# Weight sums issued one step ahead of their casts on GpSimd, in a two-branch kernel on one Trainium2 core

## The chip, the cores and the metric

The kernel runs on one core of one Trainium2 chip. The metric is the device time of one execution in microseconds (us). Five engines matter here: TensorE (PE) does the matrix products, VectorE (DVE) and ScalarE (ACT) the elementwise work on PSUM and SBUF, GpSimd (POOL) elementwise work on SBUF, and SyncE (SP) issues nearly all transfers. In the profile PEld is TensorE's weight load.

## The reference

The output is a sum of three things of shape 2048 x 512: the input, a spectral filter of its layer norm, and a mixture of 8 experts in which every expert is used (K = 8), so the routing only sets a weight per token and expert.

```python
xn = _layernorm(x)
X  = rfft2(xn) * (w_r + 1j * w_i);  A = irfft2(X)          # spectral branch, 2048 x 512
gates = softmax(xt @ wg)                                   # 8 gates per token, all kept
h = gelu(einsum("nd,edf->nef", xt, w1))                    # 8 experts, 512 -> 1792
y = einsum("nef,efd->ned", h, w2)                          # 1792 -> 512
out = x + A + einsum("ne,ned->nd", gates, y)
```

## The kernel before, in words

Precision is kept by splitting every operand of a product into a rounded high part and the remainder (low part). A high part is made by ScalarE (a cast, written CAST in the profile), the low part by a subtraction on VectorE or GpSimd that reads the source and the high part just written. A product is then three passes: high x low, low x high, high x high.

The hidden width of all experts together is cut into 56 chunks of 256. The first 8 chunks are computed plainly (`mm1`, `mm2`, lines 571 and 596) while the spectral branch runs in the background. The other 48 chunks are computed in 24 **pairs** by a Winograd-Strassen scheme, and it is this stage, from about 509 us to the end, that the change is about.

A pair `c` takes two chunks at once. Its first-layer weight, transfer `raw<-in_wa`, is cut in four blocks a11, a12, a21, a22; from these GpSimd makes four sums s1 = a21 + a22, s2 = s1 - a11, s3 (from a11 and a21) and s4 = a12 - s2 (`sums1`, line 736, through `pooled`, line 733). s3 is written over a21 and s4 over a12. Seven blocks a11, a12, s1, s2, s3, s4, a22 are then split: a cast on ScalarE and a low part on GpSimd (`split`, line 548). The tiles are called `ua..` and `us..`. The second-layer weight of the pair (`raw<-in_wb`, `sums2`, line 753) goes the same way into tiles `va..` and `vs..`.

A pair has two **units** `u = 2c + i`, one per half of the tokens (`i` = 0 and 1). In a unit, `layer1` computes seven products of weights and prepared inputs (`xr`), all by `product` at line 785, and between them ScalarE takes the gelu (line 808), VectorE adds partial results (814, 817) and multiplies by the gates (837), and the results are split again into tiles `hs` (cast 821, low part 824). The results of a unit are called h11, h12, h22 and s; their combinations feed the seven products of `layer2`, which run one unit later, in turn with the next unit's first-layer products. So in the steady state TensorE does 14 products of 12 matmuls per unit and 28 per pair. The first product of `layer2` is b22 x s4: it needs the split of h22 (the last but one of the unit's results) and the tile vs4.

The weights for the next pair of units are prepared in small steps spread over the seven rounds of a unit: in even units (`i` = 0) the v weights that this pair's `layer2` needs, in odd units the u weights of the next pair. `prepare` (line 771) is a generator; `weights(n)` (line 1096) advances it by a number of steps that a small table gives for round `n`, and each step does the sums and then the splits that the generator hands out:

```python
for step in items:
    for n, src in step:
        to[n] = pool.tile([P, 2, 2, FC], F32R, name=f"{tag}{n}")
        split(to[n], src.rearrange(...), nc.gpsimd)
    yield
```

The sums of a step stand directly ahead of the cast that reads them. The order of the instructions on each engine is a scheduler's, except where `pin` (line 545) holds it to the order in which the program was written; `strict` turns this on for the whole Strassen stage. ScalarE, VectorE, GpSimd and SyncE each work off their instructions in the order shown, so an instruction that waits holds up all behind it on that engine.

Of the kernel before, what the change touches and what calls it, by code (L numbers as in the profile page):

```python
# [11 lines left out]
F32 = mybir.dt.float32  # L12
# [16 lines left out]
F2 = 2 * FC  # L29
N2 = (E * NC - N1) // 2  # L30
# [64 lines left out]
def body(ctx: ExitStack, tc: tile.TileContext, io):  # L95
    nc = tc.nc
# [4 lines left out]
    plain, early = ExitStack(), ExitStack()  # L101
# [78 lines left out]
    last_pe, last_dve, last_act, last_pool, main_act, last_cast, last_sp = ([None] for _ in range(7))  # L180
# [361 lines left out]

    strict = False

    def pin(ins):
        return tc.keep_in_program_order(ins) if strict else ins

    def split(dst, src, eng=None):
        main_act[0] = pin(nc.scalar.copy(dst[:, 0], src)).ins  # L549
        return pin((eng or nc.vector).tensor_tensor(dst[:, 1], src, r32(dst[:, 0]), op=ALU.subtract)).ins  # L550
# [147 lines left out]
    bg, step1 = background(), iter(())  # L698
# [34 lines left out]
    def pooled(dst, a, b, op):  # L733
        pin(nc.gpsimd.tensor_tensor(dst, a, b, op=op))  # L734

    def sums1(raw, tp, early):

        a11, a12, a21, a22 = (raw[:, i * F2 : (i + 1) * F2] for i in range(4))
        s1, s2 = (tp.tile([P, F2], F32, name=n) for n in ("s1", "s2"))
        yield [("a11", a11)]  # L740
        pooled(s1, a21, a22, ALU.add)
        yield [("a12", a12)]
        pooled(s2, s1, a11, ALU.subtract)
        yield [("s2", s2)]
        pooled(a21, a11, a21, ALU.subtract)
        if early:
            yield [("s3", a21)]
        yield [("s1", s1)]
        pooled(a12, a12, s2, ALU.subtract)
        yield [("s4", a12)]  # L750
        if not early:
            yield [("s3", a21)]
        yield [("a22", a22)]

    def sums2(raw, tp, c):

        a11, a12, a21, a22 = (raw[:, i * F2 : (i + 1) * F2] for i in range(4))
        s1, s2 = (tp.tile([P, F2], F32, name=n) for n in ("s1", "s2"))
        pooled(s1, a21, a22, ALU.add)
        yield [("a11", a11)]  # L760
        pooled(s2, s1, a11, ALU.subtract)
        yield [("a12", a12)] + [("a21", a21)] * (c + 1 == N2)
        pooled(a12, a12, s2, ALU.subtract)
        yield [("s4", a12)]
        pooled(a21, a21, a11, ALU.subtract)
        yield [("s3", a21)]
        yield [("s1", s1)]
        yield [("a22", a22)]
        yield [("s2", s2)]

    def prepare(pool, tag, items, to):

        for step in items:
            for n, src in step:
                to[n] = pool.tile([P, 2, 2, FC], F32R, name=f"{tag}{n}")
                split(to[n], src.rearrange("p (k f) -> p k f", k=2), nc.gpsimd)
            yield
# [254 lines left out]
    for q in range(N1 // 2):  # L1032
        more = 2 * q + 2 < N1
        for t in range(NT):
            h = ahead_h
            for s in range(2):
# [11 lines left out]
                if t == 0 and s == 1 and not more:  # L1048
                    raw = load(io["wa"][0])
# [11 lines left out]
            if not more and t + 2 == NT:  # L1061
# [5 lines left out]
                step1 = prepare(wq, "u", sums1(raw, wq, True), w1q)  # L1067
# [11 lines left out]
    acc = keep.tile([P, 4, 2, 2, TB], F32, name="acc")  # L1079
    raw = keep.tile([P, 8 * FC], F32, name="raw")  # L1080
    step2 = prepare(rp, "v", sums2(raw, rp, 0), w2q)
    second, old, strict, rs = iter(()), [], True, {}
    for u in range(2 * N2):
        c, i = divmod(u, 2)
        if u and i == 0:
            raw = load(io["wb"][c])
            step2 = prepare(rp, "v", sums2(raw, rp, c), w2q)
        if u == 1:
            ahead.update({(n, 1): xin(n, 1) for n in ("b11", "b21", "T2")})
        if i == 1 and c + 1 < N2:  # L1090
# [24 lines left out]
        second = layer2(c, i, w2q, hs)
# [49 lines left out]
```

## Time and profile before

| | |
|---|---|
| time, median of 3 runs | 2413.72 us (2409.93 to 2417.99) |
| the profiled execution, its own time | 2409.73 us |
| its span, first to last instruction | 2407.9 us |
| mean granted TensorE clock | 0.993 |
| busy share PE / DVE / ACT / POOL | 97% / 73% / 45% / 54% |
| Strassen stage, 24 pairs | from 509 us to the end |

A row of the timeline shows the start, the time taken, engine, line, operation and tiles (buffer numbers left out), how many instructions were merged, and in brackets the time for which the engine stood idle before and what ended that. Two products that follow each other without a gap show 2.88 us each, since the end of the last matmul is modelled, but start 2.72 us apart.

### The profile page before, as it was taken

How to read it: one execution, taken by the hardware profiler on the slowest of the kernel's cores; microseconds unless marked ns; L12 is line 12 of the kernel's file. 1: busy time of each engine (PE TensorE's matmuls, PEld its weight loads, DVE VectorE, ACT ScalarE, POOL GpSimd, SP SyncE). 2: the span in 40 equal slices, each digit the busy share in tenths (PEclk: the TensorE clock that was granted, in tenths of full speed). 3: DMA queues.
4: the chain of work that ended last, by engine and by line, in shares of the span. 5: the costliest groups of instructions: out<-in, count | busy, mean ns of one | idle time of the engine just before them, and what ended most of it. 6: DMA issues, size and time to landing. Idle time of an engine off the chain costs nothing.

```text
span 2407.9 us, 28320 instructions
## 1 busy us (share of the span) xinstructions
PE 2344.9 (97%) x10736; PEld 1933.0 (80%) x10736; DVE 1755.1 (73%) x1725; ACT 1081.0 (45%) x1529; POOL 1303.0 (54%) x780
## 2 busy tenths in 40 slices
PE   9899899988999999999999999999999999999999
PEld 7687787866888888888888888888888888888878
DVE  7489669735676777777776777777776777777775
ACT  6353353325444444444444444444444444444441
POOL 2032203146765666566666666566666666566662
PEclk9999999998999999999999999999999999999999
DMA  5783532587666666666666667676666666666653
GB/s 184 268 294 117 172 115 81 173 297 253 248 231 229 239 217 243 235 246 226 227 233 225 242 218 245 231 248 225 226 231 231 242 220 243 228 249 227 226 211 120
DMA packets 119991, 530.50 MB, mean 220 GB/s; under 512 B 12176, under 2 KB 30864, under 8 KB 69040
## 3 DMA queue, kind: packets, MB, share of 16 engines
q1 hardware_dynamic: 119056, 515.99, 60.8%
q10 hardware_dynamic: 800, 12.71, 1.5%
q8 instruction: 86, 1.41, 0.2%
q14 instruction: 49, 0.40, 0.0%
HBM read 501.32 MB, written 39.92 MB: 225 GB/s over the span
## 4 chain that ended last, share of the span: by engine, by line
PE 71%; POOL 10%; DVE 9%; issue 5%; ACT 3%; DMA 2%; ACTq 0%; SPq 0%; POOLq 0%; DVEq 0%
PE B L785 23%; PE A L785 16%; PE C L785 16%; PE p L571 6%; PE p L596 5%; POOL raw L734 3%; POOL hs L824 2%; DVE hs L824 2%; DVE c L817 2%; POOL vs L550 1%; DVE c L837 1%; POOL va L550 1%; POOL s L734 1%; ACT vs L549 1%; DVE c L814 1%
## 5 line engine op out<-in xcount | busy, mean ns | idle before, releaser
L824 POOL TENSOR_TENSOR hs<-c,hs 128x1024 fp32r<-128x1024 f32 x143 | 344.6, 2410 | 305.1 <-ACT hs L821 229.4
L785 PE MATMUL C<-hs,vs 128*128 128x512 f32 x1692 | 415.8, 393 | 24.2 <-DVE hs L824 13.2
L785 PE MATMUL B<-xr,ua 128*128 128x512 f32 x1728 | 421.2, 393 | 7.1 <-DVE c L814 4.5
L785 PE MATMUL A<-xr,us 128*128 128x512 f32 x1728 | 415.5, 389 | 1.6 <-issue 1.1
L821 ACT CAST hs<-c 128x1024 fp32r<-128x1024 f32 x333 | 350.0, 1052 | 148.0 <-PE B L785 80.4
L785 PEld LDWEIGHTS C<-hs,vs 128*128 128x128 f32 x1692 | 317.2, 189 | 100.0 <-DVE hs L824 23.1
L785 PEld LDWEIGHTS B<-xr,ua 128*128 128x128 f32 x1728 | 323.4, 188 | 85.4 <-DVE c L814 16.4
L785 PEld LDWEIGHTS A<-xr,us 128*128 128x128 f32 x1728 | 324.0, 188 | 69.5 <-issue 2.4
L817 DVE TENSOR_TENSOR c<-c 128x1024 f32<-128x1024 f32 x188 | 318.4, 1694 | 0.0
L824 DVE TENSOR_TENSOR hs<-c,hs 128x1024 fp32r<-128x1024 f32 x190 | 305.5, 1628 | 9.1 <-ACT hs L821 9.1
L814 DVE TENSOR_TENSOR acc<-C,acc 128x1024 f32<-128x1024 f32 x182 | 222.1, 1220 | 92.4 <-PE C L785 92.4
L785 PE MATMUL B<-hs,va 128*128 128x512 f32 x1128 | 271.0, 389 | 0.0
L785 PEld LDWEIGHTS B<-hs,va 128*128 128x128 f32 x1128 | 211.7, 188 | 43.9
L837 DVE TENSOR_TENSOR c<-c,cwb 128x1024 f32<-128x1024 f32 x96 | 172.5, 1797 | 98.0 <-ACT c L808 98.0
L550 POOL TENSOR_TENSOR h<-c,h 128x512 fp32r<-128x512 f32 (+2 forms) x48 | 54.6, 1151 | 331.0 <-ACT h L549 230.2
L814 DVE TENSOR_TENSOR acc<-B,acc 128x1024 f32<-128x1024 f32 x92 | 112.7, 1225 | 127.1 <-PE B L785 127.1
L804 ACT COPY c<-A 128x1024 f32<-128x1024 f32 x96 | 97.5, 1016 | 229.1 <-PE A L785 229.1
L596 PE MATMUL p<-w,h 128*128 128x512 f32 x768 | 189.4, 398 | 6.9 <-DVE acc L600 4.1
L571 PE MATMUL p<-x,w 128*128 128x512 f32 x768 | 184.9, 393 | 2.7 <-ACT c L580 1.9
L808 ACT ACTIVATE c<-c 128x1024 f32<-128x1024 f32 x96 | 101.7, 1060 | 170.6 <-DVE c L814 167.9
L596 PEld LDWEIGHTS p<-w,h 128*128 128x128 f32 x768 | 144.7, 191 | 39.3 <-DVE acc L600 6.4
L550 POOL TENSOR_TENSOR va<-raw,va 128x512 fp32r<-128x512 f32 x73 | 131.0, 1794 | 72.1 <-ACT va L549 72.1
(175 smaller groups left out, 3301.9 us busy)
## 6 DMA issues: line engine op xcount, KB each, us to landing
xr<-xs_T SPq DMA_DIRECT2D x192, 1024.0 KB, 5.1
xr<-xs_b SPq DMA_DIRECT2D x144, 1024.0 KB, 4.8
cwb<-cwd SPq DMA_DIRECT2D x112, 256.0 KB, 5.2
raw<-in_wa SPq DMA_DIRECT2D x24, 1024.0 KB, 4.9
raw<-in_wb SPq DMA_DIRECT2D x24, 1024.0 KB, 4.9
tab<-cbd SPq DMA_DIRECT2D x32, 384.0 KB, 4.0
raw<-in_wp SPq DMA_DIRECT2D x16, 512.0 KB, 4.6
xs_T<-Y SPq DMA_DIRECT2D x8, 1024.0 KB, 4.7
```

Of the source, the lines that this page charges most:

```text
L550: return pin((eng or nc.vector).tensor_tensor(dst[:, 1], src, r32(dst[:, 0]), op=ALU.subtract)).ins
L571: last = nc.tensor.matmul(p1, w1[k][:, hw, f * P : (f + 1) * P], x, start=(n == 0), stop=(n == 11))
L596: last = nc.tensor.matmul(p2, h[f][:, hh, js], w2[f][:, hw], start=(n == 0), stop=(n == 6 * NFT - 1))
L734: pin(nc.gpsimd.tensor_tensor(dst, a, b, op=op))
L785: pin(nc.tensor.matmul(pt[:, m, :], w[:, hw, k, m * P : (m + 1) * P], x[:, hx, k, :], start=(start and n == 0), stop=(n == 5), skip_group_ ...
L804: last_act[0] = pin(nc.scalar.copy(dst, src)).ins
L808: last_act[0] = pin(nc.scalar.activation(v, v, AF.Gelu_apprx_tanh)).ins
L814: pin(nc.vector.tensor_add(dst, a, b))
L817: pin(nc.vector.tensor_sub(dst, a, b))
L821: main_act[0] = pin(nc.scalar.copy(hs[n][:, 0], src)).ins
L824: op = (nc.gpsimd if pool else nc.vector).tensor_tensor(hs[n][:, 1], src, r32(hs[n][:, 0]), op=ALU.subtract)
L837: pin(nc.vector.tensor_mul(dst, src, g))
```

## The change

Three things are changed in the order of the work; the arithmetic is the same.

First, a generator step may now hold a sum as well as a cast, and most sums are put one step (one round) ahead of the cast that reads them. In even units the order of the v casts is changed with it: s3 and s1 are cast in round 4 and s4 in round 5, where before s4 and s3 were cast in round 4 and s1 in round 5. Second, in the first unit (`u` = 0) the sums and casts are not pinned but left to the scheduler. Third, `pin` records its order as a dependency on the last pinned instruction of the same engine, and the wrapper `issue_after` around the steps is gone.

```diff
     def pin(ins):
-        return tc.keep_in_program_order(ins) if strict else ins
+        if strict:
+            engine = ins.ins.engine
+            if engine in pinned:
+                tc.add_manual_dep(
+                    ins.ins, pinned[engine].name,
+                    mybir.DependencyInfo(mybir.DependencyClass.NoSync, mybir.DependencyReason.DATA), reason="layout",
+                )
+            pinned[engine] = ins.ins
+        return ins
...
+    def blocks(raw, tp):
+        a11, a12, a21, a22 = (raw[:, i * F2 : (i + 1) * F2] for i in range(4))
+        s1, s2 = (tp.tile([P, F2], F32, name=n) for n in ("s1", "s2"))
+        def add(dst, a, b, op=ALU.subtract):
+            return lambda: pin(nc.gpsimd.tensor_tensor(dst, a, b, op=op))
+        parts = dict(a11=a11, a12=a12, a21=a21, a22=a22, s1=s1, s2=s2, s3=a21, s4=a12)
+        return parts, add(s1, a21, a22, ALU.add), add(s2, s1, a11), add(a12, a12, s2), add
...
     def sums1(raw, tp, early):
-        yield [("a11", a11)]
-        pooled(s1, a21, a22, ALU.add)
-        yield [("a12", a12)]
-        pooled(s2, s1, a11, ALU.subtract)
-        yield [("s2", s2)]
-        pooled(a21, a11, a21, ALU.subtract)
...
+        if early:
+            steps = ["a11", s1, s2], ["a12", s3, s4], ["s2"], ["s3"], ["s1"], ["s4"], ["a22"]
+        else:
+            steps = ["a11", s1], ["a12", s2], ["s2", s3], ["s1", s4], ["s4"], ["s3"], ["a22"]
...
     def sums2(raw, tp, c):
-        pooled(s1, a21, a22, ALU.add)
-        yield [("a11", a11)]
-        pooled(s2, s1, a11, ALU.subtract)
-        yield [("a12", a12)] + [("a21", a21)] * (c + 1 == N2)
-        pooled(a12, a12, s2, ALU.subtract)
-        yield [("s4", a12)]
-        pooled(a21, a21, a11, ALU.subtract)
-        yield [("s3", a21)]
-        yield [("s1", s1)]
-        yield [("a22", a22)]
-        yield [("s2", s2)]
+        steps = [s1], [s2, "a11"], ["a12"] + extra + [s3], ["s3"], [s4, "s1"], ["s4"], ["a22"], ["s2"]
...
         def weights(n):
-            for _ in range(((0, 0, 0, 2, 2, 2, 1) if u < 2 else (0, 1, 1, 1, 1, 2, 1) if i else (0, 0, 1, 1, 2, 2, 1))[n]):
-                with tc.issue_after(last_act[0]) if u == 0 else tc.issue_after(last_pool[0]):
-                    next(step1 if i else step2, None)
+            nonlocal strict
+            strict = u > 0
+            for _ in range(((0, 0, 1, 2, 2, 2, 1), (0, 0, 0, 2, 2, 2, 1), (0, 1, 1, 1, 2, 2, 1), (0, 1, 1, 1, 1, 2, 1))[min(u, 2 + i)][n]):
+                next(step1 if i else step2, None)
+            strict = True
```

How this moves instructions is shown at three places.

ScalarE in an even unit of the steady state, here that of pair 6 (`raw_8163` is its second-layer weight, ACTIVATE `A` the gelu of h12, ACTIVATE `c_8298` that of h22, CAST `hs_8391` the high part of h22). Before:

```order
L808 ACTIVATE A_8183<-A_8183 128x1024
L549 CAST vs4_8353<-raw_8163 128x512
L549 CAST vs3_8357<-raw_8163 128x512
L808 ACTIVATE c_8298<-c_8298 128x1024
L821 CAST hs_8391<-c_8298 128x1024
L549 CAST vs1_8393<-s1_8278 128x512
L549 CAST va22_8396<-raw_8163 128x512
```

With the change (the lines of the file are 10 higher):

```order
L818 ACTIVATE A_8185<-A_8185 128x1024
L559 CAST vs3_8353<-raw_8163 128x512
L559 CAST vs1_8357<-s1_8165 128x512
L818 ACTIVATE c_8299<-c_8299 128x1024
L831 CAST hs_8391<-c_8299 128x1024
L559 CAST vs4_8393<-raw_8163 128x512
L559 CAST va22_8396<-raw_8163 128x512
```

Ahead of the gelu of h22 there stood the casts of s4 and s3, now those of s3 and s1; s4 comes after the high part of h22.

GpSimd at the end of the plain stage, where the first pair's u weights are made (`raw_4042`) and the low part of the last hidden tile `h` of that stage in two pieces. Before:

```order
L734 TENSOR_TENSOR s1_4871<-raw_4042 128x512
L550 TENSOR_TENSOR ua11_4873<-raw_4042,ua11_4873 128x512
L550 TENSOR_TENSOR ua12_4894<-raw_4042,ua12_4894 128x512
L550 TENSOR_TENSOR h_4910<-c_4911,h_4910 128x128
L550 TENSOR_TENSOR h_4910<-c_4911,h_4910 128x384
L734 TENSOR_TENSOR s2_4872<-s1_4871,raw_4042 128x512
L734 TENSOR_TENSOR raw_4042<-raw_4042 128x512
```

With the change:

```order
L752 TENSOR_TENSOR s1_4844<-raw_4042 128x512
L752 TENSOR_TENSOR s2_4845<-s1_4844,raw_4042 128x512
L560 TENSOR_TENSOR ua11_4873<-raw_4042,ua11_4873 128x512
L560 TENSOR_TENSOR ua12_4895<-raw_4042,ua12_4895 128x512
L752 TENSOR_TENSOR raw_4042<-raw_4042 128x512
L752 TENSOR_TENSOR raw_4042<-raw_4042,s2_4845 128x512
L560 TENSOR_TENSOR h_4913<-c_4914,h_4913 128x128
L560 TENSOR_TENSOR h_4913<-c_4914,h_4913 128x384
```

The sums s2, s3 and s4 now stand ahead of the low part of `h`.

ScalarE at the start of the Strassen stage (ACTIVATE `B` is the gelu of the first unit's first result h11, `raw_5022` the first pair's second-layer weight). Before:

```order
L549 CAST us4_4983<-raw_4042 128x512
L808 ACTIVATE B_5026<-B_5026 128x1024
L804 COPY c_5082<-A_5039 128x1024
L804 COPY c_5114<-A_5039 128x1024
L808 ACTIVATE c_5114<-c_5114 128x1024
L821 CAST hs_5118<-c_5068 128x1024
L549 CAST va11_5124<-raw_5022 128x512
```

With the change:

```order
L559 CAST ua22_5000<-raw_4042 128x512
L559 CAST va11_5125<-raw_5022 128x512
L559 CAST va12_5128<-raw_5022 128x512
L559 CAST vs1_5153<-s1_5023 128x512
L559 CAST va22_5159<-raw_5022 128x512
L559 CAST vs2_5187<-s2_5024 128x512
L559 CAST vs3_5149<-raw_5022 128x512
L559 CAST vs4_5156<-raw_5022 128x512
L818 ACTIVATE B_5028<-B_5028 128x1024
```

All seven casts of the first pair's v weights now stand ahead of the first gelu, where before the first of them stood behind five other instructions. On GpSimd their sums and low parts likewise stand ahead of the first low part of `hs`, behind which they stood before.

More of the change, by code (lines that the diff above doesn't have):

```diff
@@ L543, in body @@
     strict = False
+    pinned = {}
     def pin(ins):
-        return tc.keep_in_program_order(ins) if strict else ins
+        if strict:
[7 more added lines that the diff above has]
+        return ins
     def split(dst, src, eng=None):
@@ L734, in pooled @@
         pin(nc.gpsimd.tensor_tensor(dst, a, b, op=op))
-    def sums1(raw, tp, early):
+    def blocks(raw, tp):
         a11, a12, a21, a22 = (raw[:, i * F2 : (i + 1) * F2] for i in range(4))
         s1, s2 = (tp.tile([P, F2], F32, name=n) for n in ("s1", "s2"))
-        yield [("a11", a11)]
-        pooled(s1, a21, a22, ALU.add)
-        yield [("a12", a12)]
-        pooled(s2, s1, a11, ALU.subtract)
-        yield [("s2", s2)]
-        pooled(a21, a11, a21, ALU.subtract)
-        if early:
-            yield [("s3", a21)]
-        yield [("s1", s1)]
-        pooled(a12, a12, s2, ALU.subtract)
-        yield [("s4", a12)]
-        if not early:
-            yield [("s3", a21)]
-        yield [("a22", a22)]
@@ L755, in sums2 @@
-    def sums2(raw, tp, c):
-        a11, a12, a21, a22 = (raw[:, i * F2 : (i + 1) * F2] for i in range(4))
-        s1, s2 = (tp.tile([P, F2], F32, name=n) for n in ("s1", "s2"))
-        pooled(s1, a21, a22, ALU.add)
-        yield [("a11", a11)]
-        pooled(s2, s1, a11, ALU.subtract)
-        yield [("a12", a12)] + [("a21", a21)] * (c + 1 == N2)
-        pooled(a12, a12, s2, ALU.subtract)
-        yield [("s4", a12)]
-        pooled(a21, a21, a11, ALU.subtract)
-        yield [("s3", a21)]
-        yield [("s1", s1)]
-        yield [("a22", a22)]
-        yield [("s2", s2)]
+        def add(dst, a, b, op=ALU.subtract):
+            return lambda: pin(nc.gpsimd.tensor_tensor(dst, a, b, op=op))
@@ new lines, in blocks, with sums1 @@
+        parts = dict(a11=a11, a12=a12, a21=a21, a22=a22, s1=s1, s2=s2, s3=a21, s4=a12)
+        return parts, add(s1, a21, a22, ALU.add), add(s2, s1, a11), add(a12, a12, s2), add
+    def sums1(raw, tp, early):
+        of, s1, s2, s4, add = blocks(raw, tp)
+        s3 = add(of["a21"], of["a11"], of["a21"])
+        item = {n: (n, of[n]) for n in of}
+        if early:
+            steps = ["a11", s1, s2], ["a12", s3, s4], ["s2"], ["s3"], ["s1"], ["s4"], ["a22"]
+        else:
+            steps = ["a11", s1], ["a12", s2], ["s2", s3], ["s1", s4], ["s4"], ["s3"], ["a22"]
+        return [[item.get(n, n) for n in step] for step in steps]
@@ L771, in prepare @@
+    def sums2(raw, tp, c):
+        of, s1, s2, s4, add = blocks(raw, tp)
+        s3 = add(of["a21"], of["a21"], of["a11"])
+        item = {n: (n, of[n]) for n in of}
+        extra = ["a21"] * (c + 1 == N2)
+        steps = [s1], [s2, "a11"], ["a12"] + extra + [s3], ["s3"], [s4, "s1"], ["s4"], ["a22"], ["s2"]
+        return [[item.get(n, n) for n in step] for step in steps]
     def prepare(pool, tag, items, to):
         for step in items:
-            for n, src in step:
+            for todo in step:
+                if callable(todo):
+                    todo()
+                    continue
+                n, src = todo
```

## The prediction, made before the changed kernel had run

> **What bounds the kernel now.** I read the busy shares and the windows first, then the times at which TensorE stood idle, then the other engines around those times. TensorE is the bound nearly everywhere:
>
> ```profile
> PE 2344.9 (97%) x10736; PEld 1933.0 (80%) x10736; DVE 1755.1 (73%) x1725; ACT 1081.0 (45%) x1529; POOL 1303.0 (54%) x780
> 840.00:2200.00 1360.00, 1347.84 (x5896) 1103.59 (x5895) 1024.97 (x737) 629.80 (x738) 866.11 (x494) 1.00 0.66 233
> ```
>
> So only TensorE's gaps can be won. In the 24 Strassen pairs they recur (timeline of TensorE; the first and the last of 21 equal stalls, one of them with the products around it):
>
> ```profile
> 628.40 3.02 PE L785 MATMUL B<-xr,ua 128*128 128x512 f32 x12 [0.52 <-DVE c L814]
> ...
> 709.29 2.57 PE L785 MATMUL C<-hs,vs 128*128 128x512 f32 x10 [0.59 <-DVE hs L824]
> ...
> 1015.16 3.06 PE L785 MATMUL B<-xr,ua 128*128 128x512 f32 x12
> 1018.06 0.61 PE L785 MATMUL C<-hs,vs 128*128 128x512 f32 x2
> 1019.25 2.60 PE L785 MATMUL C<-hs,vs 128*128 128x512 f32 x10 [0.58 <-DVE hs L824]
> ...
> 1024.43 2.88 PE L785 MATMUL C<-hs,vs 128*128 128x512 f32 x12
> ...
> 1051.63 2.88 PE L785 MATMUL A<-hs,vs 128*128 128x512 f32 x12
> ...
> 2259.12 2.56 PE L785 MATMUL C<-hs,vs 128*128 128x512 f32 x10 [0.61 <-DVE hs L824]
> ```
>
> A pair takes (2259.12 - 709.29) / 20 = 77.49 us. Ten products without a gap take 1051.63 - 1024.43 = 27.20, so 28 take 76.16. Each pair loses **1.33 us**, all where an odd unit begins: a little before 1015.16, where the next unit's product waits for bank B, and at 1019.25, where b22 x s4 waits after two matmuls for the low part of b22 from VectorE. What makes that late:
>
> ```profile
> 1004.96 1.29 POOL L734 TENSOR_TENSOR raw<-raw,s 128x512 f32<-128x512 f32 x1
> 1006.29 0.62 ACT L549 CAST vs<-raw 128x512 fp32r<-128x512 f32 x1 [3.76 <-POOL raw L734]
> 1007.26 1.21 DVE L814 TENSOR_TENSOR c<-B,c 128x1024 f32<-128x1024 f32 x1
> 1008.46 1.28 POOL L734 TENSOR_TENSOR raw<-raw 128x512 f32<-128x512 f32 x1
> 1009.77 0.62 ACT L549 CAST vs<-raw 128x512 fp32r<-128x512 f32 x1 [2.86 <-POOL raw L734]
> 1010.30 1.06 ACT L808 ACTIVATE c<-c 128x1024 f32<-128x1024 f32 x1
> 1011.38 1.46 DVE L837 TENSOR_TENSOR c<-c,cwb 128x1024 f32<-128x1024 f32 x1 [2.91 <-ACT c L808]
> 1012.77 1.21 DVE L814 TENSOR_TENSOR acc<-C,acc 128x1024 f32<-128x1024 f32 x1
> 1013.90 1.21 DVE L814 TENSOR_TENSOR c<-B,c 128x1024 f32<-128x1024 f32 x1
> 1015.03 1.92 DVE L817 TENSOR_TENSOR c<-c 128x1024 f32<-128x1024 f32 x1
> 1016.87 2.32 DVE L824 TENSOR_TENSOR hs<-c,hs 128x1024 fp32r<-128x1024 f32 x1
> ```
>
> The sum h22 is ready at 1007.26 + 1.21 = 1008.47. Its gelu starts only at 1010.30: ScalarE stands at the cast of s3 ahead of it, which waits for GpSimd's sum until 1009.74. From the gelu on VectorE is busy without a break down to the low part, which ends at 1019.19. The delay is 1.83 us.
>
> **The change part by part.**
>
> *Steady state.* No instruction is added or removed. In even units s3 is now summed where s4 was, and since s2 has moved to the round before, that place comes one sum (1.3) sooner: 1004.96 - 1.3 = 1003.7. It is done by 1006.3 even if it takes twice its 1.28. Its cast (0.62) then ends by 1006.9, the cast of s1, long summed, by 1007.5, and the gelu starts when h22 is there, at 1008.5. Behind it, with the durations of the rows: gate multiply 1009.6 to 1011.0, acc 1012.2. The second `c<-B,c` waits for the product that ends at 1012.2 in any case and runs to 1013.6, before bank B is wanted at 1014.92; the difference L817 to 1015.5 (as slow as now) and the low part of b22 to 1017.8. It is wanted two matmuls into the product that would start at 1017.64, at 1018.09. Without stretching it is there at 1016.0. So both waits go, with 0.3 us to spare at worst and 2.1 at best. The cast of s4 moves behind b22's high part, to about 1012.5, its low part ends by 1015: in time for 1017.64. s1 and s2 move into an idle stretch of GpSimd. Gain: 21 x 1.33 = **27.9 us**; the 0.52 and 0.14 (3.02 against 2.88) at 628.40, the same place in pair 1, **0.7**. The bounds for a pair are 0 and 1.33; I take 1.33, since 1.83 us of delay exceed it.
>
> *Last pair.* One more cast (a21) lengthens the same queue there:
>
> ```profile
> 2329.03 0.62 ACT L549 CAST vs<-raw 128x512 fp32r<-128x512 f32 x1 [2.65 <-POOL raw L734]
> 2334.42 4.61 PE L785 MATMUL B<-xr,ua 128*128 128x512 f32 x12 [1.99 <-DVE c L814]
> 2338.87 2.91 PE L785 MATMUL C<-hs,vs 128*128 128x512 f32 x12
> ```
>
> The wait of 1.99 and the slow product after it (4.61 against 2.88) both go: **3.7 us**.
>
> *End of the plain stage: a loss.* The low part of `h` is wanted by TensorE at once (on GpSimd):
>
> ```profile
> 494.32 1.29 POOL L734 TENSOR_TENSOR s<-raw 128x512 f32<-128x512 f32 x1
> 496.20 2.54 POOL L550 TENSOR_TENSOR ua<-raw,ua 128x512 fp32r<-128x512 f32 x2 [0.59 <-ACT ua L549]
> 498.71 1.43 POOL L550 TENSOR_TENSOR h<-c,h 128x128 fp32r<-128x128 f32 x2
> ```
>
> Three sums of 1.27 (2.54 for two such operations) now come first, less the 0.6 that GpSimd idled: `h` is 3.2 us later. One matmul of the next group (0.23) goes ahead of the waiting one, so TensorE stands 2.9 us more. Nothing hides it.
>
> *The first unit.* Before, GpSimd waited for the first low part of `hs` and the v weights came after it, too late for the first `layer2` product:
>
> ```profile
> 510.16 0.33 SPq L847 DMA_DIRECT2D raw<-in_wb  x1
> raw<-in_wb SPq DMA_DIRECT2D x1, 1024.0 KB, 5.3
> 521.60 3.00 PE L785 MATMUL B<-xr,us 128*128 128x512 f32 x12 [1.46 <-DMA xr<-xs_T]
> 532.56 2.40 POOL L824 TENSOR_TENSOR hs<-c,hs 128x1024 fp32r<-128x1024 f32 x1 [22.43 <-ACT hs L821]
> 536.92 3.01 PE L785 MATMUL B<-xr,ua 128*128 128x512 f32 x12 [1.97 <-DVE c L814]
> 544.07 0.62 ACT L549 CAST vs<-raw 128x512 fp32r<-128x512 f32 x1 [9.64 <-POOL raw L734]
> 550.98 1.19 PE L785 MATMUL C<-hs,vs 128*128 128x512 f32 x2 [11.04 <-ACT hs L821]
> 552.84 4.27 PE L785 MATMUL C<-hs,vs 128*128 128x512 f32 x10 [0.68 <-DVE hs L824]
> 556.95 2.91 PE L785 MATMUL B<-xr,ua 128*128 128x512 f32 x12
> ```
>
> Now GpSimd, no longer idling 0.6 us among the u weights, lets the load of the v weights go at 509.6, and it lands at 514.9 (5.3, as before). GpSimd needs six operations of 1.27 (s1, s2, two low parts, s3, s4) up to s4: 522.5. ScalarE casts s4 (0.6) and only then takes the first gelu (1.0); VectorE's gate multiply (1.2 to 1.5) follows, which frees bank B: the fifth product starts at about 525.4 instead of 521.60. The fourth ends 2.9 later than before, at 523.0, so TensorE waits 2.4. From there the ninth product is four products of 2.72, the copy out of bank A that already stood between the sixth and the seventh (1.1) and a VectorE sum (1.2) away: about 538.9 instead of 536.92. GpSimd is then done with the v weights. VectorE multiplies h22 by its gate (1.5 from 538.8), makes two differences (1.15 each, GpSimd being idle) and the low part of b22 (1.2): 543.9 instead of 552.84. Ten matmuls at full clock take 2.4, so the next product starts at 546.3 instead of 556.95: 10.7 us won, the 2.9 already paid.
>
> *The clock.* A wait can be followed by slow matmuls. 1.99 us at 2334.42 was, 1.97 at 536.92 was not, and a third:
>
> ```profile
> 381.12 5.60 PE L596 MATMUL p<-w,h 128*128 128x512 f32 x24
> 389.06 7.36 PE L596 MATMUL p<-w,h 128*128 128x512 f32 x24 [2.35 <-DVE acc L600]
> ```
>
> Its 24 matmuls took 7.36, the 24 just before 5.60: 1.8 us more. The two new waits (2.9 and 2.4) are of that size. I charge it once: 10.7 - 1.8 = **8.9 us**; the bounds are 7.1 and 10.7. [...]
>
> Sum: 27.9 + 0.7 + 3.7 + 8.9 = 41.2 us. The profiled execution took 2409.7, which gives 2368.5; the median of the runs stands 4.0 above it, so I forecast a median of **2372 us**.
>
> **The rivals.**
>
> *GpSimd and VectorE stretch each other, and the wait comes back in part.* For it: L817 took 1.92 and the low part 2.32 beside GpSimd's low parts, and those still run beside them. Against it: I have taken them at that length already. If the acc and the second `c<-B,c` stretched too, by 0.6 together, the low part would be about 0.3 late and the bank in time, so some 0.5 of the 1.33 would stay: 21 x 0.5 = 10 us lost, up to 14 if more stretches. Time 2384. [...]
>
> *The stall of the odd units is not ScalarE's queue.* If VectorE's own chain set it, only the first unit and the last pair's queue would gain: 2413.7 - 13.3 = 2400. Against it stands the break of 2.91 us in VectorE ahead of 1011.38, which ends with the gelu.
>
> *Slower: GpSimd late for b21 in odd units.* The low part of b21 and the product that reads it:
>
> ```profile
> 1028.18 2.41 POOL L824 TENSOR_TENSOR hs<-c,hs 128x1024 fp32r<-128x1024 f32 x1
> 1035.31 2.88 PE L785 MATMUL B<-hs,va 128*128 128x512 f32 x12
> ```
>
> In odd units s1 now stands ahead of the low part of b21, and waits for the transfer `raw<-in_wa` to land. If it lands late, that low part and all behind it wait, and with them the product b21 x a12, in every pair. With s1 ahead (1.3 to 2.3) the low part ends at 1032.9 at the latest and is wanted two matmuls into its product, near 1035.8. So it decides only when the transfer lands later than 1028.2 + 2.9 = 1031; the cast of a11, which reads the same transfer and stands ahead of s1, did not wait for it before. To end slower, each pair would have to lose 41/23 + 0.3 = 2.1 us; at 2.5 the time would be 2413.7 - 41.2 + 58 = 2430.
>
> **How the numbers follow.** Chances: the forecast 0.68 (own range 2362 to 2380), the stretched engines 0.15, the wrong queue 0.07, slower 0.05, and 0.05 that new waits just eat the gain. The range 2360 to 2394 takes in the forecast's clock terms, the spread of the runs (4 us each way) and the stretched engines. A difference of 0.3% (7 us) is about what a measurement of this kernel can tell from no change: faster 0.90, same 0.05, slower 0.05.
>
> **What would show it.** In the profile after: successive waits of TensorE in the steady state gone and 76.2 us a pair; ScalarE's gelu of h22 starting right when VectorE's sum ends; the last pair's slow product gone; a new wait of about 2.9 on GpSimd's `h` near 500 and one of about 2.4 on VectorE's gate multiply near 525; the first `layer2` product some 9 us sooner. The forecast is wrong if a wait of TensorE remains in each pair, or if the first unit's waits exceed those of before.

## The result, and the profile after

The changed kernel takes **2371.85 us** (median of 4 runs, 2366.85 to 2374.96) against 2412.56 us for the kernel before on the same chip: a ratio of 0.9826, 95% interval 0.9802 to 0.9851, 1.74% less. The profiled execution took 2366.85 us, 42.9 less than that of before; its span is 2365.1 us.

The busy shares of the page and the same window of the steady state as before (length; then busy time and count of PE, PEld, DVE, ACT, POOL; granted clock, DMA share, GB/s):

```profile
PE 2324.2 (98%) x10736; PEld 1931.1 (82%) x10736; DVE 1711.6 (72%) x1725; ACT 1079.7 (46%) x1529; POOL 1286.0 (54%) x780
840.00:2200.00 1360.00, 1360.00 (x6001) 1126.12 (x6000) 1009.00 (x751) 639.57 (x751) 866.29 (x500) 1.00 0.67 237
```

In this window TensorE is now busy for all of 1360.00 us, where before it was for 1347.84. ScalarE and GpSimd execute the same instructions and are nearly as busy as they were. VectorE's busy time is 43.5 us less over the whole execution, with the same 1725 instructions; most of it is in the differences `c<-c` (mean 1.42 us instead of 1.69). The place that lost 1.33 us in each pair, now (ScalarE, VectorE, GpSimd and TensorE, one fence for each engine's timeline):

```profile
988.62 0.62 ACT L559 CAST vs<-raw 128x512 fp32r<-128x512 f32 x1 [2.34 <-POOL raw L752]
...
991.97 1.06 ACT L818 ACTIVATE c<-c 128x1024 f32<-128x1024 f32 x1 [2.21 <-DVE c L824]
```

```profile
990.71 1.22 DVE L824 TENSOR_TENSOR c<-B,c 128x1024 f32<-128x1024 f32 x1 [0.36 <-PE B L795]
993.07 2.04 DVE L847 TENSOR_TENSOR c<-c,cwb 128x1024 f32<-128x1024 f32 x1 [1.13 <-ACT c L818]
...
996.16 1.22 DVE L824 TENSOR_TENSOR c<-B,c 128x1024 f32<-128x1024 f32 x1
997.29 1.87 DVE L827 TENSOR_TENSOR c<-c 128x1024 f32<-128x1024 f32 x1
999.09 2.31 DVE L834 TENSOR_TENSOR hs<-c,hs 128x1024 fp32r<-128x1024 f32 x1
```

```profile
992.73 1.29 POOL L560 TENSOR_TENSOR vs<-s,vs 128x512 fp32r<-128x512 f32 x1
996.78 1.30 POOL L560 TENSOR_TENSOR vs<-raw,vs 128x512 fp32r<-128x512 f32 x1 [2.77 <-ACT vs L559]
998.03 2.28 POOL L560 TENSOR_TENSOR va<-raw,va 128x512 fp32r<-128x512 f32 x1
```

```profile
998.67 2.88 PE L795 MATMUL B<-xr,ua 128*128 128x512 f32 x12
1001.39 2.88 PE L795 MATMUL C<-hs,vs 128*128 128x512 f32 x12
```

The sum h22 is ready at 990.71 + 1.22 = 991.93, and the gelu starts at 991.97: ScalarE now waits for VectorE's sum, and no longer for one of GpSimd's. The low part of b22 ends at 999.09 + 2.31 = 1001.40. It is wanted two matmuls (0.45) into the product of 1001.39, at 1001.84. The bank's product and this one start 2.72 us apart, so neither waits. The margin is small, 0.44 us. VectorE's gate multiply took 2.04 us here, beside GpSimd's low part of 992.73.

The sum h22 itself also comes 0.3 us sooner: it starts 0.20 us after the product that TensorE begins just before it (at 990.51), where it was 0.50 (1007.26 after 1006.76), since the difference `c<-c` ahead of it takes 1.22 us and no longer 1.95. The stall does not hang on these 0.3: with only the sums ahead (below) that difference takes 1.90 us, and the stall is gone all the same.

The last pair's slow product (4.61 us before) is gone as well:

```profile
2293.39 2.88 PE L795 MATMUL B<-xr,ua 128*128 128x512 f32 x12
```

The start of the Strassen stage (TensorE's timeline: the waits that are not as they were before, up to the product behind the first `layer2` product):

```profile
501.45 8.72 PE L606 MATMUL p<-w,h 128*128 128x512 f32 x37 [2.83 <-POOL h L560]
...
524.62 4.49 PE L795 MATMUL B<-xr,us 128*128 128x512 f32 x12 [2.39 <-POOL va L560]
...
540.06 3.04 PE L795 MATMUL B<-xr,ua 128*128 128x512 f32 x12 [1.32 <-DVE c L824]
...
544.72 2.57 PE L795 MATMUL C<-hs,vs 128*128 128x512 f32 x10 [1.17 <-DVE hs L834]
547.13 2.88 PE L795 MATMUL B<-xr,ua 128*128 128x512 f32 x12
```

The wait of 11.04 us at the first `layer2` product is gone; in its place stand the two new waits, 2.83 for the low part of `h` and 2.39 ahead of the fifth product. The product behind starts at 547.13 instead of 556.95. The second new wait is put down to GpSimd by the trace (`va`), which had nothing to do with bank B; what frees the bank is the chain of SyncE, GpSimd, ScalarE and VectorE:

```profile
508.64 0.42 SPq L857 DMA_DIRECT2D raw<-in_wb  x1
```

```profile
520.35 1.29 POOL L752 TENSOR_TENSOR raw<-raw,s 128x512 f32<-128x512 f32 x1
```

```profile
521.67 0.62 ACT L559 CAST vs<-raw 128x512 fp32r<-128x512 f32 x1 [0.63 <-POOL raw L752]
522.20 1.00 ACT L818 ACTIVATE B<-B 128x1024 f32<-128x1024 f32 x1
```

```profile
523.29 1.23 DVE L847 TENSOR_TENSOR c<-B,cwb 128x1024 f32<-128x1024 f32 x1 [12.33 <-ACT B L818]
```

The load of the v weights, the sum s4, its cast, the first gelu, the gate multiply: one behind the other, up to 524.52. This is read from the rows; the kernel with the gelu first, below, tests it.

**Where the 42.8 us of span went.** I cut both executions at the product behind the first `layer2` product (556.95 before, 547.13 after). From there to the end it was 2407.9 - 556.95 = 1850.95 us, and is 2365.1 - 547.13 = 1817.97: **33.0 less**. Up to there it is 9.8 less. Of that, 0.96 stood there already when the last matmuls of the plain stage began (the group of `L596` at 496.92 before, of `L606` at 495.96 after), ahead of everything that the change moves. So the startup gave **8.9**.

### The profile page after: what moved, and what is told of

Same layout as the page of the kernel before. It is cut to its first block, busy times and chain, and to the rows that moved or that the text cites. A ratio compares the mean times of both kernels' runs of the same rounds, so it can differ in the third digit from the quotient of the medians.

```text
span 2365.1 us, 28252 instructions
## 1 busy us (share of the span) xinstructions
PE 2324.2 (98%) x10736; PEld 1931.1 (82%) x10736; DVE 1711.6 (72%) x1725; ACT 1079.7 (46%) x1529; POOL 1286.0 (54%) x780
## 4 chain that ended last, share of the span: by engine, by line
PE 90%; DVE 3%; DMA 3%; issue 1%; POOL 1%; ACT 1%; ACTq 0%; SPq 0%; POOLq 0%; DVEq 0%
PE B L795 33%; PE A L795 22%; PE C L795 22%; PE p L581 5%; PE p L606 4%; PE psf L433 1%; PE psf L515 1%; DMA xs_T<-Y 1%; PE psf L419 1%; PE psf L527 1%; POOL w L560 0%; DMA xf<-xfd 0%; DMA tab<-cbd 0%; DMA tab<-mbd 0%; DVE T L484 0%
## 5 line engine op out<-in xcount | busy, mean ns | idle before, releaser
L834 POOL TENSOR_TENSOR hs<-c,hs 128x1024 fp32r<-128x1024 f32 x143 | 366.7, 2565 | 275.7 <-ACT hs L831 268.6
L795 PE MATMUL B<-xr,ua 128*128 128x512 f32 x1728 | 415.5, 389 | 2.2 <-DVE c L824 1.3
L795 PE MATMUL C<-hs,vs 128*128 128x512 f32 x1692 | 406.7, 389 | 1.2 <-DVE hs L834 1.2
L827 DVE TENSOR_TENSOR c<-c 128x1024 f32<-128x1024 f32 x188 | 266.9, 1420 | 0.0
L606 PE MATMUL p<-w,h 128*128 128x512 f32 x768 | 186.7, 393 | 9.8 <-POOL h L560 5.5
L606 PEld LDWEIGHTS p<-w,h 128*128 128x128 f32 x768 | 142.3, 188 | 41.9 <-DVE acc L610 7.1
L581 PEld LDWEIGHTS p<-x,w 128*128 128x128 f32 x768 | 143.8, 189 | 33.4 <-ACT x L260 2.1
```

Of the source, the lines that this page charges most:

```text
L581: last = nc.tensor.matmul(p1, w1[k][:, hw, f * P : (f + 1) * P], x, start=(n == 0), stop=(n == 11))
L606: last = nc.tensor.matmul(p2, h[f][:, hh, js], w2[f][:, hw], start=(n == 0), stop=(n == 6 * NFT - 1))
L795: pin(nc.tensor.matmul(pt[:, m, :], w[:, hw, k, m * P : (m + 1) * P], x[:, hx, k, :], start=(start and n == 0), stop=(n == 5), skip_group_ ...
L827: pin(nc.vector.tensor_sub(dst, a, b))
L834: op = (nc.gpsimd if pool else nc.vector).tensor_tensor(hs[n][:, 1], src, r32(hs[n][:, 0]), op=ALU.subtract)
```

## The experiments

In all of them the arithmetic stays as it is. To compare them, each execution is cut as above: "startup" runs from the beginning of the last group of 36 first-layer matmuls of the plain stage (488.76 before) to the product behind the first `layer2` product; "rest" from there to the end. Before, these were 68.19 and 1850.95 us; after, 59.33 and 1817.97. What lies ahead of the startup has the same instructions in all kernels, but took between 487.3 and 492.9 us; where a kernel has a single time, the two pieces say more than that time.

| kernel | startup | rest | pair |
|---|---|---|---|
| before | 68.19 | 1850.95 | 77.49 |
| the change | 59.33 | 1817.97 | 76.16 |
| the change, another execution | 62.25 | 1817.90 | 76.16 |
| even units alone | 68.09 | 1819.33 | 76.16 |
| only sums ahead | 67.66 | 1818.48 | 76.16 |
| only order of casts | 67.66 | 1819.38 | 76.16 |
| first unit alone | 59.77 | 1850.41 | 77.50 |
| gelu first | 58.05 | 1817.94 | 76.16 |
| gelu first, old u sums | 56.30 | 1817.88 | 76.16 |
| s4's cast back | 57.95 | 1821.81 | 76.3 |
| six idle copies | 57.71 | 1829.58 | 76.61 |
| eight idle copies | 59.24 | 1859.61 | 77.93 |

### Even units alone

```
 sums1, both kinds of unit:  steps as before the change
 sums2, c > 0:  [s1], [s2, "a11"], ["a12"] + extra + [s3], ["s3"], [s4, "s1"], ["s4"], ["a22"], ["s2"]
 sums2, c == 0: [s1, "a11"], [s2, "a12"] + extra, [s4, "s4"], [s3, "s3"], ["s1"], ["a22"], ["s2"]
-            strict = u > 0
...
+                with tc.issue_after(last_act[0]) if u == 0 else tc.issue_after(last_pool[0]):
```

> Only the even units from the second pair on have the new steps (sums of s3 and s4 a step ahead, s3 and s1 cast ahead of the gelu, s4 behind it); first unit, odd units and the first pair's u weights as before the change. Theory (the gelu of h22 stood behind a late sum): the whole steady gain is here, a pair takes 76.16 us instead of 77.49, no wait of TensorE from the second pair on, last pair without its slow product: 33 us less than before, about 2380 us; first `layer2` product as late as before. Rival (VectorE's own chain sets the stall, or odd units matter): a pair stays at 77.49, or comes between, and the time at 2409 or so.

Measured: 2381.01 us (median of 4) against 2410.97 us; ratio 0.9873 (0.9856 to 0.9889). The steady window and the first `layer2` product:

```profile
840.00:2200.00 1360.00, 1360.00 (x6002) 1126.50 (x6001) 1033.10 (x751) 638.38 (x751) 867.66 (x501) 1.00 0.67 237
```

```profile
554.97 1.19 PE L798 MATMUL C<-hs,vs 128*128 128x512 f32 x2 [11.10 <-ACT hs L834]
```

The whole steady gain is here, and the startup is as it was. The rest is 31.6 us shorter, not 33.0, since one wait of 1.00 us stood in the last pair of this execution; why it stood there is not shown. The new order of the sums in odd units therefore adds nothing that the steady state shows.

### One half of the edit in even units: the sums ahead, the old order of casts

```
-            steps = [s1], [s2, "a11"], ["a12"] + extra + [s3], ["s3"], [s4, "s1"], ["s4"], ["a22"], ["s2"]
+            steps = [s1], [s2, "a11"], ["a12"] + extra + [s4, s3], ["s4"], ["s3"], ["s1"], ["a22"], ["s2"]
```

(against the kernel of even units alone, for `c > 0`; the same holds for the next)

> Half of the edit in even units: the sums of s4 and s3 both stand one step ahead of their casts, but the casts ahead of the gelu remain those of s4 and s3. Theory (what counts is only that no cast ahead of the gelu waits for a sum that ends after h22 is ready): the sums end some 1.3 us or more sooner, the gelu starts when VectorE's sum ends, pair 76.16, time as with the even units whole, about 2380 us. Rival (the change of the casts' order is needed as well): pair between 76.2 and 77.49, and a wait of ScalarE on GpSimd's sum remains ahead of the gelu.

Measured: one run, 2380.29 us; rest 1818.48. ScalarE, and VectorE's sum h22:

```profile
1003.00 0.62 ACT L559 CAST vs<-raw 128x512 fp32r<-128x512 f32 x1 [0.63 <-POOL raw L752]
1005.22 1.06 ACT L821 ACTIVATE c<-c 128x1024 f32<-128x1024 f32 x1 [1.60 <-DVE c L827]
```

```profile
1003.97 1.21 DVE L827 TENSOR_TENSOR c<-B,c 128x1024 f32<-128x1024 f32 x1
```

The cast of s3 still waits for GpSimd, but only until 1003.00; h22 is ready at 1005.18, and the gelu starts at 1005.22. This wait on ScalarE ahead of the gelu cost nothing, since it ended before h22 was there.

### The other half: the order of casts, the sums directly ahead of them

```
+            steps = [s1, "a11"], [s2, "a12"] + extra, [s3, "s3"], ["s1"], [s4, "s4"], ["a22"], ["s2"]
...
-(..., (0, 1, 1, 1, 2, 2, 1), ...)
+(..., (0, 0, 1, 1, 2, 2, 1), ...)
```

> The other half: sums stay directly ahead of their casts, but s3 and s1 are cast ahead of the gelu and s4 behind it. Theory: s3's sum takes the place of s4's, one sum (1.3 us) sooner than the late one was, and the delay of 1.83 us shrinks to about 0.5, less than the 1.33 that TensorE lost plus its margin of 0.4: pair 76.16, time about 2380 us. Rival (a sum one step ahead is needed): the gelu still starts late by more than the margin, pair 76.5 to 77.49.

Measured: one run, 2379.14 us; rest 1819.38, with one wait of 0.86 us in the last pair:

```profile
1000.79 0.62 ACT L559 CAST vs<-raw 128x512 fp32r<-128x512 f32 x1 [3.63 <-POOL raw L752]
...
1003.01 1.06 ACT L821 ACTIVATE c<-c 128x1024 f32<-128x1024 f32 x1 [1.08 <-DVE c L827]
```

```profile
1001.76 1.21 DVE L827 TENSOR_TENSOR c<-B,c 128x1024 f32<-128x1024 f32 x1
```

Here too the gelu starts when h22 is ready (1002.97, 1003.01). I had expected half a microsecond of delay; it is none, since GpSimd's low part of s4 (1.50 us, and 0.73 of waiting for its cast) no longer stands ahead of s3's sum. So in the steady state the two halves of the edit do the same thing twice: either alone ends the stall. What they have in common is the theory's condition, and the rivals (order of casts needed, sums ahead needed) both fall. Only in the last pair, with its additional cast of a21, did this one still lose 0.86.

### The first unit alone

```
 sums1: steps as before the change, for all units
+        if c == 0:
+            steps = [s1], [s2, "a11"], ["a12"] + extra + [s3], ["s3"], [s4, "s1"], ["s4"], ["a22"], ["s2"]
+        else:
+            steps = [s1, "a11"], [s2, "a12"] + extra, [s4, "s4"], [s3, "s3"], ["s1"], ["a22"], ["s2"]
```

> Only the first unit has the new steps and is left to the scheduler; even and odd units later, and the u weights of the first pair, as before. Theory: the pair stays at 77.49 and the gain is the startup's alone, about 9 us (between 8 and 12), the first `layer2` product near 544 instead of 551; time about 2400 us. Since the u weights' sums are not early here, the wait of 2.8 us for `h` near 500 is absent; either the startup gains these 2.8 us more, or the wait of the fifth product grows by as much. Rival (part of the steady gain comes from the first unit): pair under 77.49.

Measured: one run, 2404.59 us, 4.6 more than expected, of which 3.8 lie ahead of the startup (it begins at 492.52 instead of 488.76); startup 59.77, 8.4 less than before, rest as before.

```profile
529.88 4.41 PE L798 MATMUL B<-xr,us 128*128 128x512 f32 x12 [5.96 <-DVE c L850]
...
704.59 2.59 PE L798 MATMUL C<-hs,vs 128*128 128x512 f32 x10 [0.62 <-DVE hs L837]
...
2254.65 2.60 PE L798 MATMUL C<-hs,vs 128*128 128x512 f32 x10 [0.60 <-DVE hs L837]
```

The pair is (2254.65 - 704.59) / 20 = 77.50. This kernel has the change's `pin` and no `issue_after`, so the third part of the change alone wins nothing in the steady state. It also settles what the 2.83 us wait for `h` costs. Without the early sums of the u weights that wait is absent, but the wait of the fifth product is 5.96 instead of 2.39: 3.57 more. The slow matmuls behind it are of one size (4.41 and 4.49). The startup is 0.4 longer than that of the change, not 2.8 shorter: the early sums gave back what they cost.

### The first gelu ahead of three casts; and with the u sums as before

The second kernel has this edit too, and beside it the early u sums undone.

```
-            strict = u > 0
-            ... (0, 0, 1, 2, 2, 2, 1) ...
+            strict = True
+            ... (3, 3, 2, 0, 0, 0, 0) ...
```

```
-            steps = ["a11", s1, s2], ["a12", s3, s4], ["s2"], ["s3"], ["s1"], ["s4"], ["a22"]
+            steps = ["a11"], [s1, "a12"], [s2, "s2"], [s3, "s3"], ["s1"], [s4, "s4"], ["a22"]
```

The gelu first:

> The changed kernel with the first unit's instructions held in written order again, and written so that the first gelu stands ahead of the casts of s3, s1 and s4. Theory (the wait of 2.39 before the fifth product of the stage is ScalarE standing at s4's cast ahead of the gelu): that wait goes, with it the slow 4.49 us of its matmuls, and the first `layer2` product stays where it was or comes sooner, 2 to 4 us less than the changed kernel. Rival (a transfer sets that product's start as well, as the 1.46 us wait for `xr` before the change had it): 0.5 to 1.5 us of the wait remain, gain under 2 us.

The gelu first, with the old u sums:

> As the one above, and the u weights' sums of the first pair where they stood before the change. Theory: the wait of 2.83 us for `h` near 501 goes too, and since the fifth product no longer hangs on the v weights nothing takes its place but the transfer of `xr` (1.3 to 1.5 us, as with only the even units changed): 1 to 2 us less than the kernel above, 3.5 to 5.5 less than the changed kernel. Rival (GpSimd, later with the v weights, makes the first `layer2` product late): no gain over the kernel above, or a loss.

The change once more:

> The changed kernel as it is, beside the two versions below, so that they can be compared on one chip: 0.982 to 0.983 of the time before.

Measured on one chip, all against 2411.04 us for the kernel before: the change as it is 2368.88 us (ratio 0.9826, 0.9812 to 0.9839), the gelu first 2369.03 (0.9823, 0.9810 to 0.9837), the gelu first with the old u sums **2365.66** (0.9811, 0.9798 to 0.9825). TensorE in the first of the two versions, then in the second:

```profile
505.65 10.05 PE L606 MATMUL p<-w,h 128*128 128x512 f32 x37 [2.82 <-POOL h L560]
...
527.60 2.88 PE L795 MATMUL B<-xr,us 128*128 128x512 f32 x12
531.85 3.00 PE L795 MATMUL A<-xr,us 128*128 128x512 f32 x12 [1.36 <-POOL vs L560]
```

```profile
521.00 2.97 PE L795 MATMUL B<-xr,us 128*128 128x512 f32 x12 [2.25 <-DMA xr<-xs_T]
525.34 3.03 PE L795 MATMUL A<-xr,us 128*128 128x512 f32 x12 [1.37 <-ACT c L814]
```

The wait of 2.39 ahead of the fifth product goes, as the theory has it, and no transfer takes its place in the first version. But the sixth product now waits 1.36 that it did not wait before: the copy out of bank A stands on ScalarE behind the cast of s4, which waits 2.13 us for GpSimd's sum. So the net is 1.0 and the slow matmuls, and the time shows none of it (2369.03 against 2368.88). The 2 to 4 us of the theory did not come; the rival's size, under 2, holds, but not by a transfer. In the second version the wait for `h` is gone, and the transfer of `xr` sets the fifth product with 2.25. Its startup is 56.30, the shortest of all, and by medians it is 3.2 us faster than the change, where 3.5 to 5.5 were expected. The intervals overlap, so from the times alone it is not shown to be better; the 3.0 us in the startup (59.33 to 56.30) are what speaks for it, and half of these are the slow matmuls (4.49 for 3.00) that it did not have. The change's own startup took 57.71 and 57.95 us where no slow matmuls fell into it (six idle copies and s4's cast back, below, which alter only later pairs), so 1.4 to 1.7 us are left as the gain.

### A late sum put back into the way: s4's cast ahead of the gelu again

```
+            steps = [s1], [s2, "a11"], ["a12"] + extra + [s3], ["s3"], [s4, "s1", "s4"], ["a22"], ["s2"]
...
-(..., (0, 1, 1, 1, 2, 2, 1), ...)
+(..., (0, 1, 1, 1, 2, 1, 1), ...)
```

> The changed kernel with one thing put back into the way of the gelu of h22 in even units (all pairs but the first): s4's cast, whose sum ends near 992.8 in the unit in which h22 is ready at 991.93. Theory: the gelu starts 1.3 to 1.5 us late, of which 0.4 is margin (b22's low part ended at 1001.40 and was wanted at 1001.84), so 0.9 to 1.1 us of stall return in each of some 22 pairs: pair 77.1 to 77.3, 20 to 25 us more than the changed kernel. Rival (more slack than the rows show, because the engines stretch one another less): pair 76.16.

Measured: one run, 2369.69 us; rest 1821.81, 3.8 more than the change, where 20 to 25 were expected. VectorE, ScalarE, GpSimd and TensorE:

```profile
990.25 1.23 DVE L827 TENSOR_TENSOR c<-B,c 128x1024 f32<-128x1024 f32 x1 [0.36 <-PE B L798]
...
999.86 1.21 DVE L837 TENSOR_TENSOR hs<-c,hs 128x1024 fp32r<-128x1024 f32 x1
```

```profile
992.85 1.06 ACT L821 ACTIVATE c<-c 128x1024 f32<-128x1024 f32 x1
```

```profile
1001.68 1.30 POOL L560 TENSOR_TENSOR vs<-s,vs 128x512 fp32r<-128x512 f32 x1 [2.82 <-ACT vs L559]
```

```profile
998.21 2.98 PE L798 MATMUL B<-xr,ua 128*128 128x512 f32 x12
```

The gelu was late as expected, by 992.85 - 991.48 = 1.37 us. But the pair lost only some 0.1 (2.98 for 2.88). The low part of b22 took 1.21 us instead of 2.31: with s4 cast earlier, GpSimd had done s4's low part earlier too and stood idle beside it, for the 2.82 us up to 1001.68. The expectation had moved VectorE's chain as one piece of fixed length. That was wrong; its length depends on what GpSimd does at the time. This kernel moves GpSimd's work as well as ScalarE's, so it does not measure what a delay alone costs.

### A delay alone: idle copies on ScalarE ahead of the gelu

Six or eight copies of a weight block that nobody reads, in all pairs but the first; they add work of no use to the computation.

```
+        def pad():
+            pin(nc.scalar.copy(spare, raw[:, 3 * F2 : 4 * F2]))
...
-        steps = [s1], [s2, "a11"], ["a12"] + extra + [s3], ["s3"], [s4, "s1"], ["s4"], ["a22"], ["s2"]
+        steps = [s1], [s2, "a11"], ["a12"] + extra + [s3], ["s3"], [s4, "s1"] + [pad] * (6 * (c > 0)), ["s4"], ["a22"], ["s2"]
```

> The changed kernel with six idle copies of 128x512 (0.53 us each) on ScalarE between the cast of s1 and the gelu of h22, in all pairs but the first; nothing moves on GpSimd. The gelu starts near 992.8 instead of 991.97, 0.85 late. Theory as I counted in the prediction (VectorE's chain behind the gelu moves as one piece, 0.4 us of margin): 0.4 us of stall in each pair, pair 76.6, about 9 us more than the changed kernel. Rival (the chain gives most of a delay back, since its operations that run beside GpSimd's get shorter when they are moved): pair 76.16.

> The same with eight copies: the gelu starts 1.9 us late, as late as before the change (1.83). Theory: 1.4 to 1.5 us of stall in each pair, pair 77.6, some 34 us more than the changed kernel, all that the steady state had won. Rival: under 1.0 us in each pair, since before the change the low part lay beside GpSimd's low parts, and here it need not.

Measured: one run each, 2381.99 and 2409.22 us. VectorE, ScalarE and TensorE with six copies:

```profile
996.08 1.22 DVE L827 TENSOR_TENSOR c<-B,c 128x1024 f32<-128x1024 f32 x1 [0.36 <-PE B L798]
999.91 1.23 DVE L850 TENSOR_TENSOR c<-c,cwb 128x1024 f32<-128x1024 f32 x1 [2.60 <-ACT c L821]
```

```profile
995.04 3.88 ACT L771 COPY spare<-raw 128x512 f32<-128x512 f32 x6
998.82 1.06 ACT L821 ACTIVATE c<-c 128x1024 f32<-128x1024 f32 x1
```

```profile
1007.59 2.52 PE L798 MATMUL C<-hs,vs 128*128 128x512 f32 x10 [0.21 <-DVE hs L837]
...
1084.20 2.53 PE L798 MATMUL C<-hs,vs 128*128 128x512 f32 x10 [0.20 <-DVE hs L837]
```

With eight:

```profile
999.31 1.22 DVE L827 TENSOR_TENSOR c<-B,c 128x1024 f32<-128x1024 f32 x1 [0.36 <-PE B L798]
```

```profile
1003.35 1.05 ACT L821 ACTIVATE c<-c 128x1024 f32<-128x1024 f32 x1
```

```profile
1012.09 2.56 PE L798 MATMUL C<-hs,vs 128*128 128x512 f32 x10 [0.64 <-DVE hs L837]
1090.02 2.53 PE L798 MATMUL C<-hs,vs 128*128 128x512 f32 x10 [0.65 <-DVE hs L837]
```

Six copies took 3.88 us, 0.65 each and not 0.53 (all write one tile; whether that is the reason no run shows), so the delays are larger than planned: 998.82 - 997.30 = 1.52 us, and 1003.35 - 1000.53 = 2.82. The pairs are 1084.20 - 1007.59 = 76.61 and 1090.02 - 1012.09 = 77.93 us, a loss of 0.45 and 1.77. The rest is 11.6 and 41.6 us longer than with the change, where 9 and 34 were expected. So 1.30 us more of delay cost 1.32 us more in each pair: between these two doses **each microsecond by which the gelu is late is one that TensorE stands**. The margin is 1.52 - 0.45 = 1.07 and 2.82 - 1.77 = 1.05 us, not 0.44. The difference is mostly the gate multiply: moved off GpSimd's low part, it took 1.23 instead of 2.04 us, 0.81 less. (0.44 + 0.81 = 1.25; TensorE starts again some 0.15 us after the low part ends, with six copies at 1007.59 after 1005.13 + 2.31 = 1007.44, which leaves 1.1.) That the kernel with six copies comes out at the 76.6 us that was expected is an accident of two errors, a delay of 1.52 for 0.85 and a margin of 1.07 for 0.4. With eight copies neither theory's number is met as stated; put at the measured delay, the slope is the theory's and the margin the rival's.

## Why the prediction was right, point by point

**The total.** The sum of 41.2 us stands against the 41.9 that the two pieces gave (33.0 and 8.9). That the median meets the forecast within 0.2 us is luck: the four runs of the changed kernel spread over 8 us, and the distance of the median from the profiled execution, taken as 4.0, was 5.0 after the change.

**The steady state, 27.9 us: right, and for the reason given.** The gelu starts 0.04 us after h22 is ready, no wait of TensorE over 0.1 us is left between 547 us and the end, and the pair is 76.16. That ScalarE's queue was the cause is shown from two sides: two different ways to have the casts out of the gelu's way before h22 is ready both end the stall, and idle copies that put the delay back (2.82 us) bring a pair of 77.93, longer than before. The rival that VectorE's own chain sets the stall is out.

**The spare margin, 0.3 at worst: right in size.** VectorE's chain from the gelu on was as slow as the worst case had it: L827 1.87 and the low part 2.31 us. The gate multiply took 2.04 us where I had 1.46. In exchange the low part was wanted 1001.84 - 991.97 = 9.87 us after the gelu's start, not 9.6. The rival of the stretched engines thus named the right danger but the wrong instructions: acc and `c<-B,c` stayed at 1.21 and 1.22, and the gate multiply, which reads two SBUF inputs as L827 does, stretched by 0.6. With 0.3 us more of it (0.44 less the 0.15 that TensorE took to start again with six idle copies) the stall would have begun to come back. Against a later gelu the margin is larger, 1.06 us by the idle copies, since the gate multiply then ran clear of GpSimd (1.23 us, from 999.91 with six copies; GpSimd's low part had ended at 999.39).

**The last pair, 3.7: right; pair 1, 0.7: a little more.** Of the 33.0 us of the rest, 27.9 are the 21 stalls. In the last pair the slow product ran 2338.87 - 2334.42 = 4.45 us up to the next one's start instead of 2.72, and stood 1.99 ahead of it, together 3.7. Of this, 0.7 is the slow clock (0.62 granted from 2334.4 to 2338.9): with the first unit alone the same wait of 2.00 was followed by a product of 3.01 and by one more wait of 0.61, 3.05 in all. Pair 1 gave 1.0: from its product at 595.08 to the one at 634.18 it was 39.10 us, and the same stretch is 38.10 now. What is left for the starts after the waits is 0.4.

**The first unit, 8.9: right in its sum.** The execution after ran 0.96 us ahead at this place, which is to be added to its times. The load goes at 508.64 + 0.96 = 509.6 (predicted 509.6), s4 ends at 522.6 (522.5), the fifth product starts at 525.6 (525.4) after a wait of 2.39 (2.4), and the product behind the first `layer2` product starts at 548.1 (546.3 and 1.8 for the clock: 548.1). The waits of 2.83 and 2.39 stand where they were put. Inside the sum small errors cancel. The fifth product came 0.2 late. Where no matmuls were slow (six idle copies) the ninth product stands 13.94 us behind the fifth, not 13.5; the terms that the prediction names for it add up to 13.2. From there to the product behind the first `layer2` product it took 7.07, not 7.4, and the slow matmuls cost 1.5, not 1.8.

**"A loss, nothing hides it": the one step that the runs correct.** The wait of 2.9 us for `h` was right as a row, and since the fifth product was worked out from the load and not from the fourth product, the sum was right as well. As a price of the early u sums it is wrong. With the first unit changed and the u sums left where they were, the fifth product waits 3.57 us longer and nothing is won (startup 59.77 against 59.33). Both ways the fifth product hangs on the v weights' load. Only where the gelu is taken out of that chain does the wait for `h` become a price, and then it is small: 58.05 against 56.30, of which about 1.4 are slow matmuls (10.05 for 37, where 8.72 is undisturbed).

**The clock, charged once with 1.8:** one of the two waits was followed by slow matmuls, 4.49 for 3.00, so 1.5. In another execution of the same kernel both were (11.56 for 8.72, and 4.58), 4.4 us together, which is more than the 3.6 at which the prediction's bounds end. The three kernels that alter only later pairs share this startup and took 57.95, 57.71 and 59.24 us, without slow matmuls, without, and with one stretch of them. So in five executions the startup gained between 5.9 and 10.5 us, and that it was 8.9 in the one compared is the draw.

**Slower, b21 late in odd units:** did not come. The rest with odd units changed (1817.97) is not longer than with even units alone (1819.33).

## What to carry to other kernels

Ahead of an instruction on the critical chain, put nothing on its engine whose input is ready later than that chain's own; whether the input is made sooner or its reader moved behind, one of the two was enough here. A delay there cost nothing up to a margin (1.06 us against a later gelu) and one for one beyond it (1.32 us for 1.30): measure the margin with idle instructions of measured length, and expect it to move when another engine's work beside the chain moves (it was 0.44 as the rows stood). A new wait ahead of a point that something else sets is not yet a loss: undo it alone before it is counted as one.

## What the runs showed of the hardware

**The same wait is followed by slow matmuls or not, as if by chance.** All kernels have the same instructions up to 488 us, among them two waits of TensorE that hardly differ between executions. After 2.68 or 2.69 us of wait near 243 us, 27 matmuls took 6.41 to 6.44 us in seven executions and 8.02 to 8.05 in five. After 2.32 to 2.35 us near 389 us, 24 matmuls took 5.73 to 5.76 in five and 7.19 to 7.36 in seven. The wait of 2.8 near 501, which six of the executions have, was followed by 8.68 to 8.72 us three times, 10.05 to 10.07 twice, and once 11.56:

```profile
388.87 5.75 PE L606 MATMUL p<-w,h 128*128 128x512 f32 x24 [2.35 <-DVE acc L610]
501.45 8.72 PE L606 MATMUL p<-w,h 128*128 128x512 f32 x37 [2.83 <-POOL h L560]
```

```profile
501.00 11.56 PE L606 MATMUL p<-w,h 128*128 128x512 f32 x37 [2.83 <-POOL h L560]
```

These are the change's two executions; the first shows, at 388.87, 5.75 for what took 7.36 before. In the slow stretches the granted clock was lower: 0.77 before the change from 389.0 to 396.4 us and 0.63 in the first execution after it from 524.6 to 529.0, against 1.00 in that one from 388.8 to 394.5 and from 501.4 to 509.0. Each slow stretch costs 1.4 to 1.6 us, once twice that, and these two places alone make up to 3.2 of the 5.6 us by which the part ahead of the startup differs between executions. What decides whether a stretch is slow is not shown; the length of the wait alone does not, since 2.35 us stood ahead of the 7.36 as of the 5.75.

**VectorE and GpSimd: the rows come out as if the two took turns.** In the rows at 993 to 1001 us above, the gate multiply (2.04 us, 1.23 alone) starts while GpSimd is at its low part of 992.73, which ends at 994.02: the 0.81 more are about the 0.95 that were left of it. The differences and low parts that follow alternate in the same way: if each starts when the other engine's operation ends and then takes its time alone (1.21 us on VectorE, 1.29 on GpSimd), L827 ends at 999.29, GpSimd's low part of 998.03 at 1000.45 and the low part of b22 at 1001.52; they ended at 999.16, 1000.31 and 1001.40. Where a VectorE operation with two SBUF inputs met a GpSimd operation of 1.3 us here, it was longer by 0.81 (the gate multiply), 0.66 (L827) and 1.10 us (the low part), and each of these was on the path behind the gelu. Operations with an input in a bank were not longer: before the change `c<-B,c` took 1.21 us at 1007.26, all of it beside GpSimd's low part of 1006.99 (1.50), and over the whole execution after the change `c<-B,c` and `c<-B,cwb` have means of 1.22 and 1.21 us, `c<-c` and `c<-c,cwb` of 1.42 and 1.85. Why the two kinds differ no run shows.
